# One weight decoder for the whole first batch, raw float32 scores for two head pairs, lower parts on VectorE

## The chip, the cores and the metric

The kernel runs on one NeuronCore of a Trainium2 chip. The metric is the device time of one execution in microseconds (us). Names in the profile: PE is TensorE, DVE is VectorE, ACT is ScalarE, POOL is GpSimd, SP is SyncE, whose queue issues most DMAs.

## What is computed

Three layers follow each other on 4608 tokens (8 batches of 576) of width 512:

```python
scores = scale * np.matmul(q, k.transpose(0, 1, 3, 2))    # 8 batches, 8 heads, 576 x 576, head_dim 64
scores = np.where(block_i >= block_j, scores, -1e9)       # blocks of 64 positions
attn = softmax(scores);  x = np.matmul(attn, v)           # -> 4608 x 512
h = (x @ w1) * (x @ w2) @ w3;  x = h @ w_out              # w1, w2: 512 x 1024 in float64
# then: a gate takes the best of 8 experts for each token, and the expert's relu(x @ e1) @ e2 is scaled by it
```

Here "layer 1" is `(x @ w1) * (x @ w2)`. w1 and w2 come in float64. TensorE takes a factor fast in the type float32r, which holds fewer bits than float32, so most factors are split into a high part (a float32r copy) and a lower part (value minus high part). A product then takes three matmuls (high by high, high by low, low by high), or two where one factor has both halves stacked in its 128 rows.

## The kernel before

**Attention.** The 64 heads are handled as 32 pairs, four to a batch. A pair is nine jobs: one for the last 64 rows of both heads together (j = 0), then for each head four jobs of 512, 384, 256 and 128 columns. The generator `attention` runs a software pipeline over n = 9 p + j. In one step it emits the scores of job n (PE, `score` or `score_f32`), the row maximum and mask of job n-1 (DVE, `rowmax`, L289), the exponential of n-2 (ACT, L297), the normalisation of n-3 (two small DVE instructions L302 and L303, then POOL, L304), the transposes of n-5 (PE, L321), their copy out of PSUM as high part (ACT, L307) and lower part (DVE, L308) of n-6, and the product with V of n-7 (PE, L351), whose result is added up on DVE (L364). After eight steps of lag `x_split` (ACT L73, POOL L74) writes the batch's x as high and lower part. With the last of these for a batch, `ready` gets the batch, at step n = 9 (4 b + 3) + 16. Each step yields twice, after its two halves.

**Raw scores.** For the first `N_RAW` = 3 pairs q and k go to TensorE as float32 (`score_f32`, L242 and L250, 64 rows): no split is made, and a matmul streams more passes. Later pairs have q and k split, by ACT (L179, L190) and POOL (L184, L195), one pair ahead, and take two float32r matmuls for a product (L267, L268, L276).

**Decoder.** `decoder` turns float64 words into float32 and splits them, one chunk of 128 x 512 after the other. One step of it, called a tick from here on, works on three chunks at a time: ACT makes the high part of the oldest (L105) and POOL its lower part (L106, value and high part both in SBUF); ACT scales the top word of the newest into a float (L114); DVE puts the remaining bits into the middle one, in three instructions (L121, L122, L124, all from SBUF). w1 and w2 are 16 chunks. Chunks 0 to 7 (`N_DEC` = 8, the first halves of the columns) are decoded while the first batch's attention runs. Chunks 8 to 15 are decoded by a second decoder, whose ticks are mixed with the first matmuls of layer 1 on batch 0, after the first batch is ready.

**Layer 1 as filler.** `layer1(b)` is 64 pieces of six matmuls (L451), each with a nominal cost of 720 ns, evacuated by ACT (L457) and by a DVE multiplication (L459). The main loop places ticks and pieces between the attention's half steps: every half step adds to `debt`, and the filler runs until it is paid. Before batch 0 is ready a half step adds 600 and a tick costs 1550, so there are ticks at every 1.3 steps. After that a step has a budget, from which the attention's own PE cost is taken: 4300 while the second decoder runs, 1850 until batch 1 is ready, and 2335 from then on. Each engine executes its instructions in the order in which they are emitted.

Of the kernel before, what the change touches and what calls it, by code (L numbers as in the profile page):

```python
# [8 lines left out]
F32 = mybir.dt.float32  # L9
# [4 lines left out]
ALU = mybir.AluOpType  # L14
# [3 lines left out]

BIG = 1e30

N_RAW, N_DEC = 3, 8

L_MAX, L_EXP, L_NRM, L_TR, L_EV, L_AV, L_XF = 1, 2, 3, 5, 6, 7, 8

# [22 lines left out]
def tile_moe_stack(ctx: ExitStack, tc: tile.TileContext, qd, kd, vd, w1, w2, w3t, wo, wg,  # L47
                   e1, e2, c_id, c_msk, c_tri, c_row, c_cst, out):
    nc = tc.nc
    NPAIR = qd.shape[0]  # L50
    B = NPAIR // 4
# [24 lines left out]
    def pool(stack, name, bufs, side="left", space=None):  # L76
        kw = dict(space=space) if space is not None else dict(side=side)
        return stack.enter_context(tc.tile_pool(name=name, bufs=bufs, reuse_waits="tile", **kw))


    def decoder(st, chunks, nraw=4, nval=4):

        n = len(chunks)
        wide = chunks[0][0].dtype != F32
        raw, val, todo = {}, {}, []

        def load(c):
            r = st.tile([128, 512, 2] if wide else [128, 512], I32 if wide else F32, tag="str", name="str", bufs=nraw)
            src = chunks[c][0]
            if wide:  # L90
                nc.sync.dma_start(out=r.rearrange("p n b -> p (n b)"), in_=src.bitcast(I32))
            else:
                nc.sync.dma_start(out=r, in_=src)
            raw[c] = r

        for c in range(min(nraw - 1, n)):
            load(c)
        yield 0
        for t in range(n + 2):
            a, b_, c = t, t - 1, t - 2  # L100
            todo = [g for g in todo if next(g, 1) is None]
            if 0 <= c < n:
                _, hi, lo, later = chunks[c]
                w_ = val.pop(c)
                nc.scalar.activation(out=hi, in_=shaped(w_, hi), func=AF.Copy)  # L105
                nc.gpsimd.tensor_tensor(out=lo, in0=shaped(w_, lo), in1=hi.bitcast(F32), op=ALU.subtract)  # L106
                if later is not None:
                    g = later(w_)
                    next(g)
                    todo.append(g)  # L110
            if a < n:
                w_ = st.tile([128, 512], F32, tag="stw", name="stw", bufs=nval)
                if wide:
                    nc.scalar.activation(out=w_, in_=raw[a][:, :, 1].bitcast(F32), func=AF.Copy, scale=2.0 ** -112)  # L114
                else:
                    nc.scalar.activation(out=w_, in_=raw.pop(a), func=AF.Copy)
                val[a] = w_
            if wide and 0 <= b_ < n:
                r = raw.pop(b_)
                wi = val[b_].bitcast(I32)  # L120
                nc.vector.tensor_scalar(out=wi, in0=wi, scalar1=3, scalar2=None, op0=ALU.logical_shift_left)  # L121
                nc.vector.scalar_tensor_tensor(out=wi, in0=r[:, :, 0], scalar=29, in1=wi,  # L122
                                               op0=ALU.logical_shift_right, op1=ALU.bitwise_or)
                nc.vector.scalar_tensor_tensor(out=wi, in0=r[:, :, 1], scalar=-2 ** 31, in1=wi,  # L124
                                               op0=ALU.bitwise_and, op1=ALU.bitwise_or)
            if a + nraw - 1 < n:
                load(a + nraw - 1)
            yield 1550
        while todo:
            todo = [g for g in todo if next(g, 1) is None]  # L130

    def shaped(t, like):
        return t if len(like.shape) == 2 else t.rearrange("p (k n) -> p k n", n=like.shape[2])
# [9 lines left out]
    wts, ready, l1_done = {}, [], []  # L143

    def x_of(b):
        return xq if (B - 1 - b) % 2 == 0 else xp
# [292 lines left out]
    def layer1(b):  # L439
        xh, xl = x_of(b)  # L440
        for f_ in range(8):
            abt = tp.tile([128, 576], F32, tag="ab", name="ab")
            for hf in range(2):
                c0 = 288 * hf
                for nm in ("w1", "w2"):
                    h_, l_ = wts[nm, f_ // 4]
                    ps = ps_m.tile([128, 512], F32, tag="mm", name="mm")
                    c = 0
                    for k_ in range(4):
                        for u, x in ((h_, xh), (h_, xl), (l_, xh)):  # L450
                            nc.tensor.matmul(ps[:, :288], lhsT=u[:, k_, f_ % 4 * 128:f_ % 4 * 128 + 128],  # L451
                                             rhs=x[:, k_, c0:c0 + 288], start=(c == 0), stop=(c == 11))
                            c += 1
                            if c == 6:
                                yield 720
                    if nm == "w1":
                        nc.scalar.activation(out=abt[:, c0:c0 + 288], in_=ps[:, :288], func=AF.Copy)  # L457
                    else:
                        nc.vector.tensor_tensor(out=abt[:, c0:c0 + 288], in0=ps[:, :288], in1=abt[:, c0:c0 + 288],  # L459
                                                op=ALU.mult)  # L460
                    yield 720
            nc.sync.dma_start(out=abT[f_ * 128:f_ * 128 + 128, b * S:(b + 1) * S], in_=abt)
        l1_done.append(b)
# [486 lines left out]
    NP = 4 * B  # L950
    seq = [(0, 4)] + [(hd, i) for hd in range(2) for i in (3, 2, 1, 0)]
    NJ = len(seq)
    NW3 = 4
    sa, sx, sm_, sw, sq = (ExitStack() for _ in range(5))
    with tc.manual_schedule():
# [10 lines left out]
        xq = tp = None  # L966

        def filler():
            nonlocal xq, tp
            ch = []  # L970
            for c in range(2):
                for nm, src in (("w1", w1), ("w2", w2)):
                    cs = slice(512 * c, 512 * c + 512)
                    for k_ in range(4):
                        ch.append((src[k_ * 128:k_ * 128 + 128, cs], wts[nm, c][0][:, k_], wts[nm, c][1][:, k_], None))
            with ExitStack() as wst:
                for c in decoder(pool(wst, "wst", 1), ch[:N_DEC], nraw=3):
                    yield c
            tp = pool(sq, "tp", 2)
            with ExitStack() as wst:  # L980
                dec = decoder(pool(wst, "wsu", 1), ch[N_DEC:], nraw=3, nval=3)
                next(dec)
                while 0 not in ready:
                    yield -1
                l1, debt = layer1(0), 0
                for c in l1:
                    yield c
                    debt += c
                    left = True
                    while debt > 0 and left:  # L990
                        left = next(dec, None) is not None
                        debt -= 1900
                    if not left:
                        break
                for _ in dec:
                    pass
            qq = pool(sq, "xqq", 1)
            xq = (qq.tile([128, 4, 576], F32R, name="xqh"), qq.tile([128, 4, 576], F32R, name="xql"))
            yield from l1
            for b in range(1, B - 1):  # L1000
                while b not in ready:
                    yield -1
                yield from layer1(b)

        fg = filler()
        done = False
        debt = 0.0
        for n, cost in at_gen:
            if n < 0:
                next(fg)  # L1010
                continue

            step = 4300 if xq is None else 1850 if 1 not in ready else 2335 if n < NP * NJ - 9 else 2000
            debt += 600 if 0 not in ready else step / 2 - cost
            while debt > 0 and not done:
                c = next(fg, None)
                if c is None:
                    done = True
                    break
                if c < 0:  # L1020
                    debt = min(debt, 0)
                    break
                debt -= c
# [7 lines left out]
        sf = ExitStack()  # L1031
        chunks, st, fw = fold_chunks(sf)
        dec = decoder(st, chunks)
        debt, ticks = 0, 8 + NW3 + 3
        for c in itertools.chain(fg, layer1(B - 1)):
# [164 lines left out]
```

## Time and profile before

| | us |
|---|---|
| median of 3 runs | 1547.42 (1547.03 to 1547.97) |
| profiled execution, its own time | 1554.69 |
| its span (first to last instruction) | 1552.9 |
| PE busy in it | 1504.0 (97%) |
| DVE, ACT, POOL busy | 947.3, 885.0, 742.6 |

The profile comes from one execution on the chip. Busy PE is a modelled figure, since matmuls are pipelined. A share over the whole span hides stages with different limits, so the stretches of the first batches are read one by one below. The stretches are cut at the row maximum of each pair's first job (9.12, 39.57, 64.00, 84.53 and 99.84 us for pairs 0 to 4) and at the end of the last `x_split` of a batch.

### The profile page before, as it was taken

How to read it: one execution, taken by the hardware profiler on the slowest of the kernel's cores; microseconds unless marked ns; L12 is line 12 of the kernel's file. 1: busy time of each engine (PE TensorE's matmuls, PEld its weight loads, DVE VectorE, ACT ScalarE, POOL GpSimd, SP SyncE). 2: the span in 40 equal slices, each digit the busy share in tenths (PEclk: the TensorE clock that was granted, in tenths of full speed). 3: DMA queues.
4: the chain of work that ended last, by engine and by line, in shares of the span. 5: the costliest groups of instructions: out<-in, count | busy, mean ns of one | idle time of the engine just before them, and what ended most of it. 6: DMA issues, size and time to landing. Idle time of an engine off the chain costs nothing. (4 is left out here: it accounts for less than half of the span.)

```text
span 1552.9 us, 28837 instructions
## 1 busy us (share of the span) xinstructions
PE 1504.0 (97%) x10623; PEld 1410.4 (91%) x10623; DVE 947.3 (61%) x2543; ACT 885.0 (57%) x1959; POOL 742.6 (48%) x727
## 2 busy tenths in 40 slices
PE   6987999999999999999999999999899999999998
PEld 3667999999999999999999999999798989889897
DVE  7588776666666666666477433347566565566551
ACT  4585876667676676676443333332456564465652
POOL 4486766656565665655233200100546464554541
PEclk9799999999999999999999999999899999999999
DMA  5333332223233223231356355654342631645510
GB/s 169 110 111 117 109 101 96 96 90 107 86 93 96 94 90 107 94 94 44 100 161 192 127 140 159 177 137 143 102 150 99 224 136 42 231 163 220 210 42 29
DMA packets 61429, 189.74 MB, mean 122 GB/s; under 512 B 9505, under 2 KB 14498, under 8 KB 58468
## 3 DMA queue, kind: packets, MB, share of 16 engines
q1 hardware_dynamic: 49060, 122.01, 25.8%
q0 software_dynamic: 12224, 65.84, 11.9%
q8 instruction: 86, 1.41, 0.4%
q14 instruction: 59, 0.48, 0.1%
HBM read 187.26 MB, written 43.01 MB: 148 GB/s over the span
## 5 line engine op out<-in xcount | busy, mean ns | idle before, releaser
L304 POOL TENSOR_SCALAR P<-P,m 128x512 f32<-128x512 f32 (+4 forms) x288 | 162.3, 564 | 193.4 <-DVE m L303 125.5
L727 DVE TENSOR_TENSOR wl<-wr,wh 128x1024 fp32r<-128x1024 f32 x128 | 189.1, 1510 | 62.8 <-ACT wh L725 56.5
L807 PE MATMUL hps<-xhl,wh 128*128 128x256 f32 x1088 | 198.2, 284 | 2.5 <-ACT xhl L796 2.1
L289 DVE CUSTOM_DVE_ANT_0 P<-s,msk 128x512 f32<-128x512 f32 (+2 forms) x320 | 151.8, 482 | 79.5 <-PE t L321 55.1
L869 PE MATMUL yps<-wh,hhw 128*128 128x512 f32 x608 | 197.4, 399 | 2.0 <-DVE hhw L833 1.9
L308 DVE TENSOR_TENSOR ptl<-t,pth 128x512 fp32r<-128x512 f32 (+3 forms) x288 | 146.3, 508 | 58.5 <-ACT pth L307 54.6
L297 ACT ACTIVATE P<-P,m 128x512 f32<-128x512 f32 (+4 forms) x288 | 167.0, 580 | 17.5 <-DVE m L289 9.8
L807 PEld LDWEIGHTS hps<-xhl,wh 128*128 128x128 f32 x1088 | 171.1, 191 | 5.1 <-ACT xhl L796 2.7
L725 ACT ACTIVATE wh<-wr 128x1024 fp32r<-128x1024 f32 x168 | 165.6, 1057 | 12.8 <-DMA wr<-e,widx 12.8
L549 PE MATMUL x<-wfh,abh 128*128 128x264 f32 (+1 forms) x576 | 163.8, 284 | 0.0
L549 PE MATMUL x<-wfl,abh 128*128 128x264 f32 (+1 forms) x576 | 162.7, 283 | 0.0
L549 PE MATMUL x<-wfh,abl 128*128 128x264 f32 (+1 forms) x576 | 162.5, 282 | 0.0
L807 PE MATMUL hps<-xhl,wl 128*128 128x256 f32 x544 | 154.8, 285 | 0.0
L321 PE MATMUL t<-ident,P 128*128 128x128 f32 x768 | 136.0, 280 | 8.5 <-DVE m L302 8.5
L869 PEld LDWEIGHTS yps<-wh,hhw 128*128 128x128 f32 x608 | 113.8, 188 | 31.1 <-DVE hhw L833 3.8
L457 ACT ACTIVATE ab<-mm 128x288 f32<-128x288 f32 x128 | 52.7, 411 | 154.5 <-PE mm L451 153.7
L307 ACT ACTIVATE pth<-t 128x512 fp32r<-128x512 f32 (+3 forms) x288 | 129.4, 449 | 5.6 <-PE t L321 2.4
L727 POOL TENSOR_TENSOR wl<-wr,wh 128x1024 fp32r<-128x1024 f32 x40 | 99.3, 2483 | 66.0 <-ACT wh L725 65.7
L351 PE MATMUL av<-pth,VV 128*128 128x256 f32 (+1 forms) x448 | 128.0, 304 | 0.7 <-ACT pth L307 0.7
L351 PE MATMUL av<-ptl,VV 128*128 128x256 f32 (+1 forms) x448 | 125.9, 303 | 1.7 <-DVE m L302 1.4
L716 POOL DMA_INDIRECT wr<-e,widx x42 | 47.1, 1122 | 152.4 <-DVE wl L727 55.4
L869 PE MATMUL yps<-wl,hhw 128*128 128x512 f32 x304 | 119.6, 394 | 0.0
(231 smaller groups left out, 4438.1 us busy)
## 6 DMA issues: line engine op xcount, KB each, us to landing
qr<-qd SPq DMA_DIRECT2D x29, 640.0 KB, 4.0
abT<-ab SPq DMA_DIRECT2D x64, 288.0 KB, 4.3
abr<-abT SPq DMA_DIRECT2D x36, 512.0 KB, 8.5
kr<-kd SPq DMA_DIRECT2D x29, 576.0 KB, 3.9
vr<-vd SPq DMA_DIRECT2D x32, 320.0 KB, 2.9
str<-w SPq DMA_DIRECT2D x16, 512.0 KB, 4.4
str<-w3t SPq DMA_DIRECT2D x16, 512.0 KB, 3.8
x2d<-row SPq DMA_DIRECT2D x7, 1026.0 KB, 8.8
```

The source lines that it names most:

```text
L289: nc.vector.tensor_tensor_reduce(out=pr[:, o_:o_ + w_], in0=s_, in1=msk[:, c_:c_ + w_], scale=-0.125, scalar=BIG, op0=ALU.add, op1=ALU.min ...
L297: nc.scalar.activation(out=pr, in_=pr, func=AF.Exp, bias=m[:, 0:1], scale=-1.0, accum_out=m[:, 3:4])
L304: nc.gpsimd.tensor_scalar(out=pr, in0=pr, scalar1=m[:, 6:7], scalar2=1.0, op0=ALU.mult, op1=ALU.mult)
L307: nc.scalar.activation(out=dst_h, in_=src, func=AF.Copy)
L308: nc.vector.tensor_tensor(out=dst_l, in0=src, in1=dst_h.bitcast(F32), op=ALU.subtract)
L321: nc.tensor.transpose(t_[:, 128 * c:128 * c + 128], pr[:, 128 * c:128 * c + 128], ident)
L351: nc.tensor.matmul(t_[:, x0:n], lhsT=vv[:, k_, hd, :], rhs=pt[:, hd, o_ + x0:o_ + n], start=(c == 0), stop=(c == 2 * kcs - 1))
L549: nc.tensor.matmul(ps[:, :c1 - c0], lhsT=u[:, k_, j * 128:j * 128 + 128], rhs=w_[:, k_, c0:c1], start=(c == 0), stop=(c == 23))
L725: nc.scalar.activation(out=h_[:, sl], in_=rawt[i % 2][:, sl], func=AF.Copy)
L727: (nc.gpsimd if c == 1 and not pre else nc.vector).tensor_tensor(out=l_[:, sl], in0=rawt[i % 2][:, sl], in1=h_[:, sl].bitcast(F32), op=ALU ...
L807: nc.tensor.matmul(ps[:, d], lhsT=u[:, f2, k_, 128 * d:128 * d + 128], rhs=x[:, k_], start=(k_ == 0 and c == 0 and (s > 0 or d == 0)), sto ...
L869: nc.tensor.matmul(ps, lhsT=u[:, g, o_], rhs=w_[:, g * 512:g * 512 + 512], start=(c == 0), stop=(c == 23))
```

## The change

- `N_RAW` is 2: pair 2 has its q and k split like all later pairs, with two ACT copies and two POOL subtractions for each of q and k during pair 1, and float32r scores.
- There is one decoder for all 16 chunks, with three buffers (`nval=3`) where the first had four, and it runs wholly before batch 0 is ready.
- In it the lower part is made by DVE (`on_dve`), behind the three instructions of the same tick, and no longer by POOL. The later decoder, of w3 and w_out, is as it was.
- The budgets are changed: a half step adds 400 before batch 0 is ready; from then on a step has 2335, also in the second batch.

```diff
-N_RAW, N_DEC = 3, 8
+N_RAW = 2
...
-    def decoder(st, chunks, nraw=4, nval=4):
+    def decoder(st, chunks, nraw=4, nval=4, on_dve=False):
...
-                w_ = val.pop(c)
+                w_ = done = val.pop(c)
                 nc.scalar.activation(out=hi, in_=shaped(w_, hi), func=AF.Copy)
-                nc.gpsimd.tensor_tensor(out=lo, in0=shaped(w_, lo), in1=hi.bitcast(F32), op=ALU.subtract)
+                if not on_dve:
+                    nc.gpsimd.tensor_tensor(out=lo, in0=shaped(w_, lo), in1=hi.bitcast(F32), op=ALU.subtract)
...
+            if on_dve and 0 <= c < n:
+                nc.vector.tensor_tensor(out=lo, in0=shaped(done, lo), in1=hi.bitcast(F32), op=ALU.subtract)
             if a + nraw - 1 < n:
                 load(a + nraw - 1)
             yield 1550
...
-                for c in decoder(pool(wst, "wst", 1), ch[:N_DEC], nraw=3):
+                for c in decoder(pool(wst, "wst", 1), ch, nraw=3, nval=3, on_dve=True):
                     yield c
             tp = pool(sq, "tp", 2)
-            with ExitStack() as wst:
-                dec = decoder(pool(wst, "wsu", 1), ch[N_DEC:], nraw=3, nval=3)
-                next(dec)
-                while 0 not in ready:
-                    yield -1
-                l1, debt = layer1(0), 0
-                for c in l1:
-                    yield c
-                    debt += c
-                    left = True
-                    while debt > 0 and left:
-                        left = next(dec, None) is not None
-                        debt -= 1900
-                    if not left:
-                        break
-                for _ in dec:
-                    pass
             qq = pool(sq, "xqq", 1)
             xq = (qq.tile([128, 4, 576], F32R, name="xqh"), qq.tile([128, 4, 576], F32R, name="xql"))
-            yield from l1
-            for b in range(1, B - 1):
+            for b in range(B - 1):
                 while b not in ready:
                     yield -1
                 yield from layer1(b)
...
-            step = 4300 if xq is None else 1850 if 1 not in ready else 2335 if n < NP * NJ - 9 else 2000
-            debt += 600 if 0 not in ready else step / 2 - cost
+            step = 800 if 0 not in ready else 2335 if n < NP * NJ - 9 else 2000
+            debt += step / 2 - (cost if 0 in ready else 0)
```

On DVE, the start of pair 2 stood like this before. `P<-s,msk` 128x288 are the two row maxima of the pair's first job, `xf<-av,xf` and `ptl<-t,pth` belong to earlier jobs:

```order
L289 ISA P,m<-s,msk 128x288
L289 ISA m 128x1
L292 TENSOR_TENSOR m<-m 128x1
L364 TENSOR_TENSOR xf<-av,xf 64x320
L308 TENSOR_TENSOR ptl<-t,pth 128x128
L302 TENSOR_SCALAR m<-m 128x1
L303 RECIPROCAL m<-m 128x1
```

At the same place of the changed kernel there is a tick between them (`stw` is the value under construction, `w11l` a lower part of w1; line numbers are those of the changed kernel):

```order
L292 ISA P,m<-s,msk 128x288
L292 ISA m 128x1
L295 TENSOR_TENSOR m<-m 128x1
L122 TENSOR_SCALAR stw<-stw 128x512
L123 SCALAR_TENSOR_TENSOR stw<-str,stw 128x512
L125 SCALAR_TENSOR_TENSOR stw<-str,stw 128x512
L128 TENSOR_TENSOR w11l<-stw,w11h 128x512
L367 TENSOR_TENSOR xf<-av,xf 64x320
L311 TENSOR_TENSOR ptl<-t,pth 128x128
L305 TENSOR_SCALAR m<-m 128x1
```

Four DVE instructions have come in, and such a group stands at every second job of pairs 0 to 2. Counted on DVE at the first row maximum of pairs 1, 2, 3 and 4, the ticks begun were 7, 8, 8 and 8 before and are 5, 9, 14 and 16 now; the lower parts made on DVE are 4, 8, 13 and 16.

Behind the end of the first batch, DVE had this before, at the second head of pair 4 (`ab<-mm,ab` is layer 1's multiplication):

```order
L289 ISA P,m<-s,msk 128x256
L289 ISA m 128x1
L121 TENSOR_SCALAR stw<-stw 128x512
L122 SCALAR_TENSOR_TENSOR stw<-str,stw 128x512
L124 SCALAR_TENSOR_TENSOR stw<-str,stw 128x512
L459 TENSOR_TENSOR ab<-mm,ab 128x288
L308 TENSOR_TENSOR ptl<-t,pth 128x3x128
L121 TENSOR_SCALAR stw<-stw 128x512
L122 SCALAR_TENSOR_TENSOR stw<-str,stw 128x512
L124 SCALAR_TENSOR_TENSOR stw<-str,stw 128x512
L459 TENSOR_TENSOR ab<-mm,ab 128x288
```

and has this now:

```order
L292 ISA P,m<-s,msk 128x256
L292 ISA m 128x1
L311 TENSOR_TENSOR ptl<-t,pth 128x3x128
L462 TENSOR_TENSOR ab<-mm,ab 128x288
L305 TENSOR_SCALAR m<-m 128x1
L306 RECIPROCAL m<-m 128x1
```

The ticks are gone from there, and fewer pieces of layer 1 stand in the same steps. By the first job of pair 8 (the end of the second batch) DVE has made 13 of layer 1's multiplications in both orders.

On POOL, the first jobs had a lower part of a weight between nearly all normalisations (`P<-P,m`):

```order
L205 TENSOR_TENSOR VV<-vr,VV 128x10x64
L106 TENSOR_TENSOR w10l<-stw,w10h 128x512
L304 TENSOR_SCALAR P<-P,m 128x576
L106 TENSOR_TENSOR w10l<-stw,w10h 128x512
L304 TENSOR_SCALAR P<-P,m 128x512
L304 TENSOR_SCALAR P<-P,m 128x384
L106 TENSOR_TENSOR w10l<-stw,w10h 128x512
```

They are now followed, in pair 1, by the splits of pair 2's q and k:

```order
L307 TENSOR_SCALAR P<-P,m 128x256
L187 TENSOR_TENSOR X<-qr,X 64x640
L307 TENSOR_SCALAR P<-P,m 128x128
L187 TENSOR_TENSOR X<-qr,X 64x640
L307 TENSOR_SCALAR P<-P,m 128x576
L307 TENSOR_SCALAR P<-P,m 128x512
L198 TENSOR_TENSOR K_448<-kr,K_422 128x576
```

The lower parts of the weights have left POOL, and four subtractions for pair 2 have come to it.

## Rows read from the trace of the kernel before

**Rows 1.** The page: span, and busy time by engine

```profile
span 1552.9 us, 28837 instructions
PE 1504.0 (97%) x10623; PEld 1410.4 (91%) x10623; DVE 947.3 (61%) x2543; ACT 885.0 (57%) x1959; POOL 742.6 (48%) x727
```

**Rows 2.** Stretches: length, busy us and count by engine, granted clock, DMA

```profile
9.12:39.57 30.45, 23.40 (x54) 12.79 (x54) 26.98 (x64) 17.37 (x41) 15.68 (x16) 1.00 0.49 147
39.57:64.00 24.43, 23.92 (x78) 14.96 (x79) 15.21 (x56) 14.03 (x38) 12.46 (x16) 0.89 0.51 147
64.00:84.53 20.53, 20.02 (x79) 12.89 (x80) 12.92 (x53) 14.71 (x40) 11.21 (x14) 0.72 0.19 61
84.53:99.84 15.31, 11.83 (x79) 9.98 (x78) 13.14 (x53) 14.53 (x40) 13.84 (x17) 1.00 0.31 104
99.84:112.50 12.66, 9.99 (x64) 8.05 (x62) 11.36 (x44) 11.63 (x30) 11.74 (x15) 1.00 0.29 86
112.50:214.60 102.10, 93.50 (x687) 90.66 (x688) 82.80 (x252) 73.98 (x190) 68.50 (x72) 0.98 0.38 119
214.60:306.60 92.00, 92.00 (x701) 91.00 (x699) 58.54 (x228) 64.03 (x173) 55.97 (x64) 1.00 0.28 96
```

**Rows 3.** Timeline of POOL, start and duration: last x_split of batch 0

```profile
111.75 0.73 POOL L74 TENSOR_TENSOR xpl<-xf,xph 128x256 fp32r<-128x256 f32 x1 [0.37 <-ACT xph L73]
```

**Rows 4.** Groups by line, DVE, 9.12 to 112.5 us: busy, mean ns, idle before

```profile
L122 DVE SCALAR_TENSOR_TENSOR stw<-str,stw 128x512 int32<-128x512 int32 x8 | 7.9, 984 | 0.3
L124 DVE SCALAR_TENSOR_TENSOR stw<-str,stw 128x512 int32<-128x512 int32 x8 | 7.4, 930 | 0.3
...
L121 DVE TENSOR_SCALAR stw<-stw 128x512 int32<-128x512 int32 x8 | 5.4, 671 | 0.4 <-ACT stw L114 0.4
```

**Rows 5.** Timeline of DVE: the first tick, and one instruction of the second

```profile
12.07 0.43 DVE L121 TENSOR_SCALAR stw<-stw 128x512 int32<-128x512 int32 x1 [0.38 <-ACT stw L114]
12.54 0.69 DVE L122 SCALAR_TENSOR_TENSOR stw<-str,stw 128x512 int32<-128x512 int32 x1
13.26 0.69 DVE L124 SCALAR_TENSOR_TENSOR stw<-str,stw 128x512 int32<-128x512 int32 x1
...
14.94 1.64 DVE L122 SCALAR_TENSOR_TENSOR stw<-str,stw 128x512 int32<-128x512 int32 x1
```

**Rows 6.** Timeline of POOL beside it

```profile
14.69 1.34 POOL L106 TENSOR_TENSOR w10l<-stw,w10h 128x512 fp32r<-128x512 f32 x1 [5.09 <-ACT w10h L105]
```

**Rows 7.** Tile abl on DVE, the whole span: ns min/median/max

```profile
  L74 DVE TENSOR_TENSOR abl<-abr,abh x56: 675/692/1587, 836.2 to 1048.6; 128x512 fp32r<-128x512 f32 x56
```

**Rows 8.** Groups by line, DVE, 112.5 to 150 us: the second decoder's ticks

```profile
L122 DVE SCALAR_TENSOR_TENSOR stw<-str,stw 128x512 int32<-128x512 int32 x8 | 10.2, 1274 | 0.3
L124 DVE SCALAR_TENSOR_TENSOR stw<-str,stw 128x512 int32<-128x512 int32 x8 | 8.7, 1088 | 0.3
L121 DVE TENSOR_SCALAR stw<-stw 128x512 int32<-128x512 int32 x8 | 6.2, 776 | 0.0
```

**Rows 9.** Groups by line, POOL, 9.12 to 112.5 us: splits of q and k

```profile
L184 POOL TENSOR_TENSOR X<-qr,X 64x640 fp32r<-64x640 f32 x6 | 9.3, 1546 | 0.2
L195 POOL TENSOR_TENSOR K<-kr,K 128x576 fp32r<-128x576 f32 x6 | 8.5, 1419 | 0.0
```

**Rows 10.** Timeline of PE, float32 scores of pairs 1 and 2

```profile
39.35 2.07 PE L242 MATMUL s<-K,X 64*128 64x512 f32 x2
...
57.60 3.29 PE L250 MATMUL s<-K,X 64*128 64x288 f32 x8
...
63.78 2.07 PE L242 MATMUL s<-K,X 64*128 64x512 f32 x2
...
75.65 1.12 PE L242 MATMUL s<-K,X 64*128 64x512 f32 x2
...
81.62 1.31 PE L276 MATMUL s<-K,X 128*128 128x288 f32 x8
```

**Rows 11.** Stretch of 2 us, as in rows 2

```profile
60.00:62.00 2.00, 2.00 (x6) 1.24 (x6) 0.00 (x0) 0.21 (x2) 1.92 (x3) 0.50 0.07 8
```

## The prediction

> **What bounds the kernel now.** I read the page first, then the stretches around the changed code, then the single instructions in them. Over the whole span PE is busy 97% and DVE 61% [rows 1], so a saving on DVE, ACT or POOL alone looks worthless. But the change acts on the first 215 us, and there the limits differ [rows 2]. In pair 0 (30.45 us) DVE is busy 26.98 us and PE 23.40: DVE is the bound, with seven decoder ticks. In pairs 1 and 2 PE is busy 23.92 of 24.43 us and 20.02 of 20.53, while DVE has 15.21 and 12.92: PE is the bound, with raw float32 scores. In pair 3, with split scores and no tick, the time is 15.31 us, with ACT at 14.53, POOL at 13.84 and DVE at 13.14, all nearly full. The eight jobs up to the end of the first batch take 12.66 us more. The first batch is ready when its last lower part is written, at 111.75 + 0.73 = 112.5 us [rows 3]. The second batch takes 102.1 us, the third, without ticks, 92.0 us with PE busy throughout [rows 2]. That is one reading: behind the first batch layer 1 fills PE, and the second batch loses 102.1 - 92.0 = 10.1 us because the second decoder's ticks stand between the attention's instructions on DVE (82.80 us busy against 58.54).
>
> So the time is: when the first batch is ready, plus what the second one loses, plus a remainder that is bound by PE and holds the same work in both kernels. The order supports this, since DVE has made 13 of layer 1's multiplications at the start of pair 8 in both.
>
> **The price of a tick on DVE.** Undisturbed, its three instructions take 0.43 + 0.69 + 0.69 = 1.81 us [rows 5]. The mean of the eight in the first batch is 0.984 + 0.930 + 0.671 = 2.58 us [rows 4], that of the eight behind it 1.274 + 1.088 + 0.776 = 3.14 us [rows 8]. The difference is POOL. In the second tick L122 takes 1.64 instead of 0.69 us, and POOL's lower part runs from 14.69 to 16.03 us, from before it to 0.55 us before its end [rows 5, 6]. The Trainium skill (SBUF — State Buffer, "Who interferes with whom") has the rule for that: VectorE and GpSimd share a pair of ports under an exclusive lock, and an instruction with two SBUF inputs on VectorE blocks for the whole of a GpSimd one that holds it. This trace agrees, with 1.64 against 0.69 us. The sum by the rule alone is the first rival below.
>
> The new lower part on DVE has a row of its own kind elsewhere: both operands in SBUF, 128x512, 0.692 us at the median [rows 7]. A tick then costs 1.81 + 0.69 = 2.50 us if POOL never interferes. At most I set 3.14 + 0.69 = 3.83. In pair 0 POOL loses its lower parts and keeps mostly short normalisations; I take 1.9 us for the three and 0.69 for the fourth. From pair 1 on it has the splits of q and k, 1.55 and 1.42 us each [rows 9], now one pair sooner; I take 3.1 us for the four, nearer to the low end because the lower part itself was the usual blocker in rows 4.
>
> **The first batch, pair by pair.** The first row maximum stays at 9.12 us (the loads and the scores of pair 0 are the same).
> - Pair 0: 30.45 - 7 x 2.58 = 12.4 us without ticks. Now five ticks and four lower parts: 5 x 1.9 + 4 x 0.69 = 12.3. Together 24.7 us (24.2 to 28.0).
> - Pair 1: four ticks in place of one. DVE needs 15.31 + 4 x 3.1 = 27.7 us. PE's side hangs on the clock. The row of 60 to 62 us shows 0.50, that is 1.2 GHz [rows 11]. At that level a first score of 512 columns takes 2.07 us, and 1.12 after the rise [rows 10]. The one at 39.35 us also took 2.07, so the low level held there too, though the stretch is printed as 0.89. One pair wholly at 1.2 GHz is (63.78 - 57.60) + 2 x (75.65 - 63.78) = 29.9 us of PE; with the clock as it was, 24.43. Since PE will be emptier than before, I expect it low for most of the pair, and take 28.5 us (24.4 to 32, the upper end with 2 us for steps in which both are waited for in turn).
> - Pair 2: five ticks, and PE has the split scores, so DVE is the bound: 15.31 + 5 x 3.1 = 30.8. PE's gain (eight matmuls in 1.31 instead of 3.29 us at the pair's start [rows 10]) is hidden by that. ACT's added copies are hidden too: with seven ticks in pair 0 it was busy 17.37 us of 30.45 [rows 2]. I take 30 us, since some of the ticks fall into the 15.31 - 13.14 = 2.2 us in which DVE was not busy. Bounds: 13.14 + 5 x 2.5 = 25.6, and 15.31 + 5 x 3.83 = 34.5.
> - Pair 3: two ticks and a third lower part: 15.31 + 2 x 3.1 + 0.7 = 22.2 us (21.0 to 23.7).
> - The eight jobs behind it: 12.66 us as before.
>
> Ready at 9.12 + 24.7 + 28.5 + 30 + 22.2 + 12.66 = 127.2 us instead of 112.5: 14.7 us later. The ends give 117.0 (4.5 later) and 140.0 (27.5 later).
>
> **The second batch.** Without ticks and with the budget of 2335 from its first step it is the kind of batch that took 92.0 us: -10.1 us. Its rate can be no better, as PE had no idle time there. I add 1 us for the clock: a mean of 0.98 over 102.1 us [rows 2] is about 2 us of lost PE time, and PE may now come out of the first batch at the low level (0 to 2 us).
>
> **Sum.** 14.7 - 10.1 + 1 = +5.6 us. On the profiled execution, with 1554.69 us of its own and a span of 1552.9, that is 1560.3 and 1558.5. It lies 7.3 us above the median of the runs, a difference that I take as the same for both kernels: 1547.4 + 5.6 = 1553.0 us. The likeliest case's own range is 1550 to 1558. SP's and the DMA's part costs nothing: a tick's load has three buffers and ticks are two steps apart, over 5 us.
>
> **Rivals.**
> - *The port is freed.* POOL's lower part, which cost DVE's ticks up to 1 us each, is gone, and the subtraction costs 0.69 us, so a tick with everything in it is 2.50 us. Pair 0 is then 24.2, pair 1 15.31 + 10 = 25.3, pair 2 27.8, pair 3 21.0: ready at 120.1 us, 7.6 later, and the sum is 7.6 - 10.1 + 1 = -1.5: 1545.9 us. For it: the undisturbed ticks in rows 5. Against it: the splits of q and k on POOL stay and come earlier, and pair 1's scores are still raw. Chance 0.2.
> - *TensorE was the bound of pairs 1 and 2, and the ticks fall into DVE's waits* (faster). DVE was idle for 24.43 - 15.21 = 9.2 and 20.53 - 12.92 = 7.6 us there. If PE's clock rises as early as before (24.4 us for pair 1), pair 2's cheaper scores take PE away as its limit, and the ticks fit at 2.5 us into the idle time: 9.12 + 24.2 + 24.4 + 25.6 + 21.0 + 12.66 = 117.0, 4.5 later; 4.5 - 10.1 = -5.6: 1541.8 us. It decides if the first batch is ready before 119.5 us. Against it: DVE's work in pair 2 alone, with five ticks, exceeds the 20.53 us that the pair took. Chance 0.17.
> - *The ticks stay blocked.* POOL's splits meet most ticks, at 3.83 us each, and pair 1 runs wholly at 1.2 GHz: 9.12 + 28 + 32 + 34.5 + 23.7 + 12.66 = 140.0, and +27.5 - 10.1 + 2 = +19.4: 1566.8 us. Against it: the mean in rows 4 with POOL's lower part in every tick is only 2.58. Chance 0.1. The same side has the case that the second batch's 10 us come from layer 1 behind attention and do not return in full; half of them gone is +10.7, 1558.1 us. Chance 0.08.
>
> **How the numbers follow.** The forecast has 0.45. About 0.2% (3.1 us) is what can be told from no change. Slower by more: nearly all of the forecast (its lower part lies within), and both late cases, 0.59. Within: most of the first rival and the edges of its neighbours, 0.22. Faster: the second rival and the low edge of the first, 0.19. The range from 1544 to 1563 leaves the full second rival (1541.8) and the full third one out, with some 0.2.
>
> **What would show it.** Right: the last `x_split` of batch 0 between 122 and 133 us; DVE busy above 85% in pairs 0, 2 and 3; the second batch 92 to 94 us long; ticks in pairs 2 and 3 of about 3.1 us with POOL's splits beside the long ones; in pair 1, first scores of 512 columns near 2.07 us. Wrong: ready before 119.5 us, or DVE's waits for PE's transposes in pair 2 as long as before, or a second batch that keeps 100 us though no tick is in it.

## The result and the profile after

The changed kernel takes 1563.62 us in the median of four runs (1563.39 to 1566.09) against 1547.22 us before: the ratio is 1.0105, with an interval of 1.0084 to 1.0126. It is slower by 16.4 us, where 5.6 were forecast; the direction was right and the size was not. The median also lies 0.6 us above the stated range of 1544 to 1563 us.

The page of the changed kernel answers to [rows 1]:

```profile
span 1561.8 us, 28838 instructions
PE 1506.1 (96%) x10623; PEld 1418.2 (91%) x10623; DVE 958.5 (61%) x2559; ACT 884.7 (57%) x1963; POOL 724.7 (46%) x715
```

Its profiled execution took 1563.55 us, like its other runs. The one of the kernel before, on which the prediction rests, took 1554.69 us and was 7.3 us above the median of that kernel's runs. So the kernel before was profiled again, unchanged, as the first experiment (`b0_look`, 1548.74 us). Its stretches, cut as in [rows 2] at the first row maximum of pairs 0 to 4 and at the last `x_split` of batches 0 to 2 (length, then busy us and count of PE, PEld, DVE, ACT and POOL, granted clock, DMA):

```profile
8.90:39.40 30.50, 23.45 (x54) 12.76 (x54) 26.93 (x64) 17.36 (x41) 15.69 (x16) 1.00 0.50 151
39.40:61.50 22.10, 21.59 (x78) 13.37 (x79) 15.22 (x57) 13.94 (x38) 11.02 (x16) 1.00 0.57 148
61.50:77.30 15.80, 15.06 (x79) 9.97 (x79) 13.59 (x54) 14.45 (x40) 12.63 (x15) 1.00 0.32 101
77.30:92.50 15.20, 11.73 (x79) 9.91 (x78) 13.08 (x53) 14.42 (x40) 13.76 (x17) 1.00 0.31 105
92.50:105.20 12.70, 10.01 (x64) 8.07 (x62) 11.38 (x46) 11.63 (x30) 11.76 (x15) 1.00 0.28 83
105.20:208.70 103.50, 95.18 (x687) 92.34 (x687) 82.69 (x252) 73.87 (x190) 68.27 (x72) 0.97 0.37 118
```

The same stretches of the changed kernel:

```profile
8.70:33.20 24.50, 23.24 (x55) 12.82 (x54) 21.71 (x61) 14.69 (x37) 6.70 (x9) 1.00 0.74 232
33.20:62.20 29.00, 23.74 (x78) 15.75 (x79) 26.27 (x69) 20.16 (x50) 14.70 (x17) 0.63 0.44 136
62.20:92.30 30.10, 19.36 (x80) 16.23 (x78) 27.38 (x73) 19.66 (x50) 14.29 (x16) 0.62 0.43 126
92.30:119.30 27.00, 18.55 (x77) 15.71 (x78) 22.53 (x64) 16.16 (x42) 15.69 (x18) 0.62 0.19 59
119.30:131.90 12.60, 9.97 (x64) 8.00 (x62) 11.32 (x44) 10.84 (x29) 9.45 (x13) 1.00 0.25 76
131.90:224.40 92.50, 91.73 (x692) 90.36 (x692) 61.20 (x230) 64.11 (x172) 55.80 (x66) 1.00 0.32 92
```

Two things are to be read here. Against its own usual execution the change moves the end of the first batch from 105.2 to 131.9 us (+26.7) and shortens the second batch from 103.5 to 92.5 us (-11.0), so batch 1 is ready 15.7 us later; the spans differ by 1561.8 - 1547.0 = 14.8 us. And the profile in [rows 2] differs from this second one mainly in pairs 1 and 2: 24.43 and 20.53 us there, at a clock of 0.89 and 0.72, against 22.10 and 15.80 us here, at 1.00. Executions of the kernel before spread from 1544 to 1561 us, and the first profile was one of the longer ones.

The clock column has a trap. The profile prints 1.00 up to its first record of the clock, which stands at 51.7 us in `b0_look`, at 33.6 us in the changed kernel and at 14.3 us in `a_warm12` below. A float32 score of 512 columns took 2.07 us at 39.18 us in `b0_look`, as at the recorded 0.50, and 1.12 us at 61.26 us. So the 1.00 of pair 0 in both tables, and of pair 1 of `b0_look` up to 51.7 us, is no measured level.

In the changed kernel it is DVE that is busy nearly throughout in pairs 1 and 2 (26.27 of 29.00 us, 27.38 of 30.10), and the clock is 0.63 and 0.62. Who waited for whom in pair 2 (62.2 to 92.3 us; us in total, times, longest us):

```profile
DVE P L292 <- PE t L324: 3.2, 2, 1.9
...
PE av L354 <- DVE m L305: 5.3, 3, 2.4
PE t L324 <- DVE m L305: 4.3, 4, 3.3
```

PE waited 9.6 us for DVE's small instructions there, and DVE 3.2 us for PE. In pair 1 it is 4.1 us against none, in pair 3 7.3 us against 2.7. The ticks, by groups, in its whole first batch (8.7 to 131.9 us; busy, mean ns of one, idle before):

```profile
L123 DVE SCALAR_TENSOR_TENSOR stw<-str,stw 128x512 int32<-128x512 int32 x16 | 15.4, 960 | 0.6
L125 DVE SCALAR_TENSOR_TENSOR stw<-str,stw 128x512 int32<-128x512 int32 x16 | 12.3, 769 | 0.5
L122 DVE TENSOR_SCALAR stw<-stw 128x512 int32<-128x512 int32 x16 | 11.7, 734 | 0.5 <-ACT stw L115 0.5
L128 DVE TENSOR_TENSOR w21l<-stw,w21h 128x512 fp32r<-128x512 f32 x4 | 3.0, 748 | 0.7 <-ACT w21h L105 0.7
L128 DVE TENSOR_TENSOR w11l<-stw,w11h 128x512 fp32r<-128x512 f32 x4 | 2.7, 684 | 0.0
```

The three old instructions take 2.46 us in the mean, 2.58 in [rows 4], though POOL's lower part is gone; the new one takes 0.68 to 0.75 us, as in [rows 7].

### The profile page after: what moved, and what is told of

It reads as the page before. It is cut to its first block, busy times and chain, and to the rows that moved or that the text cites. A ratio compares the mean times of both kernels' runs of the same rounds, so it can differ in the third digit from the quotient of the medians.

```text
span 1561.8 us, 28838 instructions
## 1 busy us (share of the span) xinstructions
PE 1506.1 (96%) x10623; PEld 1418.2 (91%) x10623; DVE 958.5 (61%) x2559; ACT 884.7 (57%) x1963; POOL 724.7 (46%) x715
## 3 DMA queue, kind: packets, MB, share of 16 engines
q1 hardware_dynamic: 49188, 122.63, 26.7%
q8 instruction: 86, 1.41, 0.4%
## 5 line engine op out<-in xcount | busy, mean ns | idle before, releaser
L292 DVE CUSTOM_DVE_ANT_0 P<-s,msk 128x512 f32<-128x512 f32 (+2 forms) x320 | 152.0, 482 | 78.7 <-PE t L324 46.5
L300 ACT ACTIVATE P<-P,m 128x512 f32<-128x512 f32 (+4 forms) x288 | 166.7, 579 | 20.2 <-DVE m L292 15.7
L354 PE MATMUL av<-ptl,VV 128*128 128x256 f32 (+1 forms) x448 | 129.8, 311 | 11.2 <-DVE m L305 10.9
L354 PE MATMUL av<-pth,VV 128*128 128x256 f32 (+1 forms) x448 | 129.7, 307 | 2.5 <-ACT pth L310 2.5
L730 POOL TENSOR_TENSOR wl<-wr,wh 128x1024 fp32r<-128x1024 f32 x40 | 99.4, 2485 | 67.0 <-ACT wh L728 66.7
L324 PEld LDWEIGHTS t<-ident,P 128*128 128x128 f32 x768 | 98.4, 146 | 27.3 <-issue 22.2
```

The lines of the kernel that those rows point to most:

```text
L292: nc.vector.tensor_tensor_reduce(out=pr[:, o_:o_ + w_], in0=s_, in1=msk[:, c_:c_ + w_], scale=-0.125, scalar=BIG, op0=ALU.add, op1=ALU.min ...
L300: nc.scalar.activation(out=pr, in_=pr, func=AF.Exp, bias=m[:, 0:1], scale=-1.0, accum_out=m[:, 3:4])
L324: nc.tensor.transpose(t_[:, 128 * c:128 * c + 128], pr[:, 128 * c:128 * c + 128], ident)
L354: nc.tensor.matmul(t_[:, x0:n], lhsT=vv[:, k_, hd, :], rhs=pt[:, hd, o_ + x0:o_ + n], start=(c == 0), stop=(c == 2 * kcs - 1))
L730: (nc.gpsimd if c == 1 and not pre else nc.vector).tensor_tensor(out=l_[:, sl], in0=rawt[i % 2][:, sl], in1=h_[:, sl].bitcast(F32), op=ALU ...
```

## The experiments

Two theories stood against each other. **D**: DVE is the bound of the first batch, and each tick moved there is paid. **C**: TensorE is emptier between ticks, its clock stays at 1.2 GHz, and that makes pairs 1 to 3 long.

**b0_look**, the kernel before once more.

> The kernel before, unchanged, profiled once more, because its first profiled execution (1554.69 us) was 7.3 us above the median of its runs. Theory 1 (the clock of TensorE in pairs 1 and 2 differs from execution to execution): this one is near 1547 us, the first batch is ready some 5 to 8 us earlier than 112.5 us, near 105 to 107, and the stretch at 1.2 GHz from 58 to 75 us is shorter or absent. Rival (the surplus lay elsewhere, in the experts or their transfers): ready again at 112.5 us, and the 7 us are missing behind 800 us.

1548.74 us, ready at 105.2 us. In the first profile the clock fell within pair 1 and rose again within pair 2; here it stayed high from 51.7 to 123 us. So the 7.3 us lay in pairs 1 and 2, as expected. What makes the clock fall in one execution and not in another is not shown.

**One part at a time.**

```diff
 d_only (changed kernel)
-N_RAW = 2
+N_RAW = 3
-    decoder(pool(wst, "wst", 1), ch, nraw=3, nval=3, on_dve=True)
+    decoder(pool(wst, "wst", 1), ch, nraw=3, nval=3)
 v_only (kernel before, both decoders)
-    nc.gpsimd.tensor_tensor(out=lo, ...)
+    nc.vector.tensor_tensor(out=lo, ...)   # behind the three DVE instructions of the tick
 r_only (kernel before)
-N_RAW, N_DEC = 3, 8
+N_RAW, N_DEC = 2, 8
```

> One decoder for all 16 chunks and the new budgets alone; three raw pairs, lower parts on POOL. Theory 1 (more ticks in the first batch are the whole loss, wherever the lower part is made): ready near 130 to 136 us, 1561 to 1568 us. Rival (the loss is mostly the lower parts on DVE): ready near 120 us, 1550 to 1554 us.

> The lower parts of both of the first two decoders on DVE, and nothing else. Theory 1 (POOL's lower part blocks DVE for about as long as the subtraction takes there): the same as before or up to 4 us less, 1543 to 1548 us, the ticks' three old instructions at 1.9 to 2.2 us instead of 2.58. Rival (16 x 0.69 us more on an engine that is the bound): 1552 to 1558 us.

> Two raw pairs instead of three, and nothing else. Theory 1 (TensorE was the bound of pair 2 through its raw scores): pair 2 takes 15 to 17 us instead of 20.5, 1542 to 1545 us. Rival (ACT and POOL are full there, and the splits of q and k come earlier): pair 1 gets longer by what pair 2 loses, 1546 to 1549 us.

Against 1547.64 us of the kernel before, taken beside it, `d_only` took 1562.08 us (ratio 1.0085, 1.0066 to 1.0105), ready at 129.7 us and with a second batch of 92.4 us, about as its theory 1 said. `v_only` took 1551.15 (1.0005, 0.9979 to 1.0031) and `r_only` 1550.1 (1.0013, 0.9997 to 1.0028): neither can be told from no change, and both medians lie outside both of their ranges. In its profile pair 2 of `r_only` took 15.3 us, as expected; but with raw scores it took 15.8 us in `b0_look`, where the clock was up, so there was little to gain. So the loss is in the single decoder with its budgets, wherever its lower parts are made. `d_only` with POOL's lower parts has ticks of 954 + 989 + 1058 ns = 3.00 us for three instructions, the changed kernel 2.46 + 0.70 = 3.16 us for four. `v_only` is the cleaner comparison, as only the lower part moves: its three instructions took 0.47 + 0.76 + 0.85 = 2.08 us in the first batch, against 2.58 [rows 4], and the fourth 0.68. So the subtraction on DVE costs about what POOL's blocking did, or 0.2 us more.

**The clock by itself.**

```diff
 a_warm12 (changed kernel; b_warm6: kernel before, 6 instead of 12)
+        def spin(p, st):
+            for _ in range(12 if p < 4 else 0):
+                nc.tensor.matmul(st[:, :256], lhsT=tri[:, 0:128], rhs=tri, start=True, stop=True)
                 st = ps_s.tile([128, 512], F32, tag="s", name="s")
+                spin(p, st)      # in score and score_f32, one-head jobs
```

> The changed kernel with twelve spare bf16 matmuls of 256 columns ahead of each one-head score of pairs 0 to 3, into the PSUM tile that the score then overwrites, so that TensorE has work where it waited. Theory D (DVE's ticks bound the first batch, the low clock of TensorE only adds a few us): the clock is high in pairs 2 and 3, and the batch is ready at 123 to 127 us, 1554 to 1559 us. Theory C (the low clock is what made pairs 1 to 3 long): ready at 118 us or before, 1545 to 1551 us. If the clock does not rise, TensorE becomes the bound and it takes over 1570 us.

> The kernel before with six such spare matmuls ahead of each one-head score of pairs 0 to 3. Theory C: the clock rises before 51 us and stays, pair 1 takes 16 to 19 us instead of 22 to 24, ready at 98 to 102 us, 1539 to 1544 us, with less spread than the 1545 to 1560 us of the kernel before. Theory D (the clock matters little next to DVE and ACT): 1545 to 1549 us, or up to 1553 us if the spare matmuls are in the way.

`a_warm12` took 1570.11 us (1.0146, 1.0116 to 1.0177). Its pairs 0 to 3, in the columns of the stretches above:

```profile
8.80:37.00 28.20, 27.51 (x162) 18.28 (x162) 21.65 (x62) 16.24 (x39) 6.42 (x9) 1.00 0.63 198
37.00:65.00 28.00, 24.90 (x165) 18.11 (x166) 26.45 (x71) 18.45 (x46) 13.56 (x16) 1.00 0.45 140
65.00:95.40 30.40, 24.57 (x187) 21.95 (x185) 28.88 (x74) 20.59 (x51) 15.74 (x17) 0.94 0.42 128
95.40:121.30 25.90, 22.47 (x162) 20.14 (x162) 22.56 (x64) 15.81 (x41) 14.61 (x18) 0.87 0.17 57
```

The clock is 1.00 in pair 1 and 0.94 in pair 2, and these pairs take 28.0 and 30.4 us, against 29.0 and 30.1 at 0.63 and 0.62. DVE is about as busy as without the spare matmuls (26.45, 28.88 and 22.56 us in pairs 1 to 3, 26.27, 27.38 and 22.53 without), and waits for PE at most 0.8 us in any of them. With the clock up nothing is gained, so C falls as the main cause; pair 3 got 1.1 us shorter. The batch was ready at 134.3 us, 2.4 us later than without: pair 0, at 27.51 us of PE, took 28.2 us instead of 24.5, which is the spare matmuls' doing. The span grew by 4.2 us; where the rest of that came in is not shown. `b_warm6` took 1554.12 us (1.0038, 1.0017 to 1.0058): the clock was up from 42 to 127 us, but pair 1 took 22.3 us as without, and pairs 2 and 3 got longer (19.9 and 16.2 us). With its spare matmuls PE was busy for 22.35, 19.89 and 15.91 us of these pairs, so it was their bound, and the run says little about the clock alone. Both miss theory C's numbers, and both miss D's too: `a_warm12` is 11 us above D's 1559 us and was ready 7 us after its 127 us, `b_warm6` is 1 us above what D allowed. What speaks against C is the stretches and the waits, not the times.

**Less work for DVE.**

```diff
 a_bits (changed kernel): L122 and L123 are left out
-                nc.vector.tensor_scalar(out=wi, in0=wi, scalar1=3, ...)
-                nc.vector.scalar_tensor_tensor(out=wi, in0=r[:, :, 0], scalar=29, in1=wi, ...)
 a_1200 (changed kernel)
-            step = 800 if 0 not in ready
+            step = 1200 if 0 not in ready
```

> The changed kernel without the first two of the three DVE instructions of each of the 16 ticks (the low bits of w1 and w2 are left as the scaling made them, so the weights are wrong in value). That takes 16 x 1.1 to 1.9 us from DVE in the first batch. Theory D: ready 18 to 28 us earlier, at 104 to 114 us, 1537 to 1546 us. Theory C: the clock stays low all the same, pairs 1 and 2 then wait for TensorE (29 and 22 us), and ready comes only 8 to 14 us earlier, 1550 to 1556 us.

> The changed kernel with the ticks of the first batch at the old spacing (budget 1200 instead of 800), so that all 16 are done in pair 2. Theory D: DVE's work is the same, pairs 0 to 2 get longer and pair 3 returns to 15 to 20 us: ready at 126 to 130 us, 1558 to 1562 us. Theory C: a pair without ticks runs densely, the clock rises in it, and ready comes at 120 to 125 us, 1552 to 1557 us.

`a_bits` took 1546.69 us (1542.66 to 1547.90), ready at 112.3 us, that is 19.6 us earlier, in D's range and outside C's; its median is 0.7 us above the 1546 that D gave. The two instructions had 15.4 + 11.7 = 27.1 us in the changed kernel's first batch, so some 70% of what DVE lost came off the time. Its first pairs:

```profile
31.10:55.40 24.30, 22.50 (x79) 15.10 (x79) 20.14 (x61) 19.99 (x50) 12.75 (x15) 0.65 0.41 139
55.40:78.00 22.60, 14.39 (x78) 12.34 (x77) 20.82 (x64) 18.82 (x48) 15.80 (x15) 0.86 0.50 163
```

Pair 1, with raw scores and a clock of 0.65, is now nearer to PE's limit (22.50 of 24.30 us). `a_1200` took 1559.7 us (1.0070, 1.0043 to 1.0098), ready at 127.1 us; pairs 1 to 3 took 36.1, 22.8 and 16.8 us. The ticks moved, and the time went with them; D's ranges held the time, the ready point and pair 3. D also had pair 2 longer, and it got shorter, 22.8 instead of 30.1 us, since only two ticks begin in it.

**What lengthens a tick.**

```diff
 a_raw5 (changed kernel)
-N_RAW = 2
+N_RAW = 5
```

> The changed kernel with five raw pairs, so that POOL splits no q and k while ticks run. Theory L (POOL's splits of q and k are what lengthens the ticks beyond 2.5 us): the four DVE instructions of a tick take 2.5 to 2.7 us in the mean of pairs 1 to 3, against 3.3, 3.0 and 4.0 us in the changed kernel. Rival (normalisations or something else lengthen them): above 3.0 us. The time is no help here, since the raw scores hold pairs 2 and 3 at 28 to 31 us where the clock is low: 1561 to 1572 us.

Ticks in pairs 1 to 3 (33.1 to 117.8 us) of `a_raw5`, where POOL splits q or k once instead of 13 times:

```profile
L125 DVE SCALAR_TENSOR_TENSOR stw<-str,stw 128x512 int32<-128x512 int32 x11 | 8.8, 802 | 0.4
L123 DVE SCALAR_TENSOR_TENSOR stw<-str,stw 128x512 int32<-128x512 int32 x11 | 8.2, 742 | 0.4
L122 DVE TENSOR_SCALAR stw<-stw 128x512 int32<-128x512 int32 x11 | 5.5, 502 | 0.0
```

and of the changed kernel (33.2 to 119.3 us):

```profile
L123 DVE SCALAR_TENSOR_TENSOR stw<-str,stw 128x512 int32<-128x512 int32 x11 | 10.4, 946 | 0.4
L122 DVE TENSOR_SCALAR stw<-stw 128x512 int32<-128x512 int32 x11 | 9.1, 831 | 0.0
L125 DVE SCALAR_TENSOR_TENSOR stw<-str,stw 128x512 int32<-128x512 int32 x11 | 8.8, 805 | 0.4
```

The three instructions take 2.05 us nearly without splits and 2.58 with them, so with the lower part of 0.70 us 2.75 and 3.3 us: the splits cost some 0.5 us a tick. 2.75 us is just above the theory's range, and the undisturbed 1.81 us [rows 5] are not reached. What lengthens the ticks by the other 0.2 us is not shown. The kernel took 1563.09 us in one run: what the ticks gained, the raw scores took.

**Other orders around the second batch.**

```diff
 b_2335 (kernel before)
-            step = ... else 1850 if 1 not in ready else 2335 ...
+            step = ... else 2335 ...
 best_p (kernel before; best_v: with v_only's edit too)
-            step = 4300 if xq is None
+            step = 9000 if xq is None
-                        debt -= 1900
+                        debt -= 2300
 n_dec12 (kernel before)
-N_RAW, N_DEC = 3, 8
+N_RAW, N_DEC = 3, 12
```

> The kernel before with the budget of 2335 instead of 1850 in the rest of the second batch; its ticks stay. Theory D (the ticks on DVE cost the second batch its 10 us, the budget nothing): the second batch stays at 101 to 104 us, 1545 to 1549 us. Rival B (the small budget costs it): 93 to 97 us, 1537 to 1542 us.

> The kernel before with more of layer 1 around the second decoder's ticks (a tick for every 2300 of layer 1's cost instead of 1900, and a budget of 9000 instead of 4300 while they run), so that fewer attention steps compete for DVE there. Theory D: the second batch loses 4 to 7 us instead of 10 to 11, 1541 to 1545 us. Rival (layer 1's pieces are held by their own evacuations, or attention is late afterwards): 1547 us or more.

> The same with the lower parts of both decoders on DVE. Theory D: the ticks of the second decoder get shorter by POOL's blocking (the second batch took 100.4 us instead of 103.5 with that alone), 1538 to 1543 us. Rival: no better than best_p, 1543 to 1547 us.

> The kernel before with 12 chunks in the first decoder and 4 in the second; pace, budgets and lower parts as before. Theory D (a tick costs about 3.3 us in the first batch, where DVE is the bound, and about 1.4 us in the second, where layer 1 covers a part): half of the whole change, ready 12 to 15 us later than with 8, at 117 to 120 us from 105.2 (up to 7 us more where the clock stays low in pairs 1 and 2), the second batch 97 to 99 us, 1553 to 1557 us. Rival (the loss comes from the slow pace and the budgets of the single decoder, not from where the ticks stand): ready before 112 us, 1544 to 1549 us.

`b_2335` took 1557.21 us (1.0039, 1.0012 to 1.0067): its second batch was 107.5 us long, 4 to 5 us longer than with the small budget. That lies outside both ranges. So the small budget did not cost the second batch its 10 us; by elimination the ticks are left. But `b_2335` moved something else too: layer 1 on batch 0 ended at 200.4 us, 18.5 us before the second batch, and PE was busy for only 14.41 us of that rest. In the kernel before it ended 0.6 us behind the second batch. How far the spread of layer 1 over the batch sets its length was not tested by itself. `best_p` (1548.88; 1.0001, 0.9978 to 1.0024) and `best_v` (1549.76; 1.0003, 0.9981 to 1.0025) are equal to the kernel before within what can be told. Their profiles show second batches of 103.2 and 99.4 us: `best_p` shows nothing of the 4 to 7 us that D let one expect, and `best_v` little more than the 100.4 us of `v_only`. Both times miss D's ranges. That of `best_p` fits its rival; that of `best_v` is above its rival's, too. None of the versions beats the kernel before beyond its spread.

`n_dec12` took 1552.8 us (1.0016, 0.9991 to 1.0042), not surely slower. Its stretches from pair 1 to the end of batch 1:

```profile
39.50:71.70 32.20, 26.18 (x78) 16.05 (x79) 25.57 (x69) 17.57 (x45) 18.13 (x20) 0.61 0.56 159
71.70:92.50 20.80, 20.29 (x79) 13.13 (x80) 12.96 (x54) 14.69 (x40) 11.22 (x14) 0.71 0.19 60
92.50:107.70 15.20, 11.73 (x79) 9.89 (x78) 13.07 (x53) 14.42 (x40) 13.73 (x17) 1.00 0.32 105
107.70:120.30 12.60, 10.02 (x64) 8.09 (x62) 11.27 (x44) 11.64 (x30) 11.69 (x14) 1.00 0.29 84
120.30:213.00 92.70, 87.41 (x644) 85.19 (x645) 70.95 (x238) 68.24 (x179) 62.88 (x69) 0.98 0.33 105
```

The five ticks in pair 1 make it 32.2 us. Ready at 120.3 us lies where D put it for a low clock in pairs 1 and 2 (0.61 and 0.71), and outside the rival's range; the time is 0.2 us below D's. The second batch, at 92.7 us, is shorter than D said, but only 644 matmuls ran in it, against 687: 43 were left for later, and the last multiplication of layer 1 on batch 0 began at 223.8 us, 10.8 us behind the batch. So half of the move costs less than half of the loss, and the price of a tick is not the same for each one moved.

## Why the prediction was wrong

**Where it held.** First row maximum 8.7 us (9.12 forecast), pair 0 24.5 (24.7), pair 1 29.0 (28.5), pair 2 30.1 (30), the eight jobs at the end 12.6 (12.66), the second batch 92.5 us (92.0 + 1). The mechanism was the right one: DVE took the bound, which `a_bits`, `a_warm12` and the waits in pair 2 show, and the second batch gave back its loss. The clock in pair 1 was low from 40.5 us on, as assumed for most of the pair (first scores of 512 columns took 1.41 and 2.07 us), but `a_warm12` shows that this was not what set the pair's length. Two of the hits are partly luck. Pair 1 had 27.7 us for DVE, and the 0.8 us on top were for a clock that did not set its length. In pair 0 the three instructions took 2.20 us a tick instead of 1.9, so the rest of the pair was shorter than the 12.4 us worked out for it, and the two errors cancelled. Of the signs of being right, one failed: DVE was busy for 83% of pair 3, not above 85%.

**The step that failed most** is the one from the profiled execution to the runs: "It lies 7.3 us above the median of the runs, a difference that I take as the same for both kernels". For the changed kernel it is -0.1 us (1563.55 against 1563.62). In that execution of the kernel before the batch was ready 7.3 us later than in `b0_look`, 7.1 us of it in pairs 1 and 2, where PE was the bound and ran at the low clock from 58.6 to 75.6 us. In the changed kernel DVE sets the length of these pairs, so they hold no such surplus to take off again. With 105.2 us in place of 112.5, the same working gives 127.2 - 105.2 = 22.0 later, less 103.5 - 92.0 = 11.5, plus 1: +11.5 us.

**The second term** is pair 3: 27.0 us, where 15.31 + 2 x 3.1 + 0.7 = 22.2 were forecast. Its ticks on DVE and the small instruction that waits like them (changed kernel, timeline, start and duration):

```profile
93.22 1.48 DVE L295 TENSOR_TENSOR m<-m 128x1 f32<-128x1 f32 x1
...
96.12 1.79 DVE L122 TENSOR_SCALAR stw<-stw 128x512 int32<-128x512 int32 x1
...
103.59 1.79 DVE L123 SCALAR_TENSOR_TENSOR stw<-str,stw 128x512 int32<-128x512 int32 x1
...
119.26 0.46 DVE L292 CUSTOM_DVE_ANT_0 P<-s,msk 128x288 f32<-128x288 f32 x1 [2.71 <-PE t L324]
```

and POOL beside them:

```profile
93.15 1.53 POOL L187 TENSOR_TENSOR X<-qr,X 64x640 fp32r<-64x640 f32 x1
...
96.08 1.54 POOL L187 TENSOR_TENSOR X<-qr,X 64x640 fp32r<-64x640 f32 x1
...
103.24 1.58 POOL L198 TENSOR_TENSOR K<-kr,K 128x576 fp32r<-128x576 f32 x1
```

Each of the three long DVE instructions begins beside a split on POOL and ends at its end or within 0.6 us of it. The Trainium skill's rule of the exclusive lock (SBUF — State Buffer, "Who interferes with whom") fits that: L123 and L295 read two operands from SBUF. Of `tensor_scalar`, which L122 is, that section of the Trainium skill says that it can take the shared ports too, in a two-port mode. In which mode L122 ran no run here shows. The two ticks of pair 3 took 3.85 and 4.02 us instead of 3.1. L295 took 1.48 us for one column, 1.2 us more than the 0.24 us that the same instruction (then L292) took at the start of pair 3 before. The third lower part took 0.95 us and was waited for 0.74 us. And at the pair's end DVE waited 2.71 us for PE, which was busy throughout from 116.0 to 119.3 us at a clock of 0.55, mostly 1.2 GHz. Together that is more than the 4.8 us; the 2.2 us in which DVE was not busy in the 15.31 took up a part, and how the terms share the rest no run separates. With a higher clock (`a_warm12`) the pair still took 25.9 us.

**The sum.** 5.6 forecast, 7.3 of the wrong base, and 3.3 by which the spans of the two first profiles differ more than forecast (1561.8 - 1552.9 = 8.9) make 16.2 of the measured 16.4 us. The 3.3 us are 4.7 of the first batch (131.9 - 127.2, nearly all of it pair 3) less 0.5 in the second batch (92.5 - 102.1 = -9.6 where -9.1 was forecast) and 0.9 behind it.

**The rivals.** That the freed port makes ticks cheap (2.50 us) fell with the means above, 3.2 us; that they hide in DVE's waits fell with pair 2, which took 30.1 us. The late rival had the right side for the wrong reason: its ticks of 3.83 us were met only in pair 3 (3.9 us in the mean). That half of the second batch's gain stays away did not occur.

## What to carry to other kernels

Work moved between stages has a price in each: here some 70% of what DVE's ticks took came on top in a stage that DVE bounds (`a_bits`), and taking them away gave back 11 us in one where TensorE had other work beside them. Before a sum is built on one profiled execution, see that its time is near the median of the runs; if it is not, find the stretch that differs before anything else. Moving an instruction from POOL to DVE to take away a conflict costs its own length there: in `v_only` it took 0.5 us of blocking off a tick and put 0.68 us on it. And where POOL then does other work beside the ticks, as with the splits of q and k here, the blocking comes back (2.58 us for the three instructions in pairs 1 to 3, as in [rows 4]).

## What the runs showed of the hardware that was not expected

- One and the same kernel gave 28 executions from 1545.4 to 1561.5 us on one core. Two profiles of it, 7.3 us apart at the end of the first batch, differ in the granted clock of pairs 1 and 2 (0.89 and 0.72 against 1.00 and 1.00; after the first record, at 51.7 us in both, it fell to 1.2 GHz from 58.6 to 75.6 us in the one and not in the other). TensorE was busy nearly throughout these pairs in both.
- With spare matmuls the granted clock was 1.00 in pair 1 and 0.94 in pair 2, where it was 0.63 and 0.62 without, and these two pairs were 1.0 us shorter and 0.3 us longer.
- A DVE instruction on one column with both operands in SBUF (L295) took 1.48 us beside a split on POOL of 1.53 us; at the same place of the kernel before it took 0.24 us.
